# Fill products, per-pair transposes, a halved last product and placed casts in a planned attention and channel-mix kernel

## The chip, the cores and the metric

The kernel runs on one core of a Trainium2 chip. The metric is the device time of one execution in microseconds (us). A core has five engines that work side by side, each through its own queue in order: TensorE (PE, whose weight loads are listed as PEld), VectorE (DVE), ScalarE (ACT), GpSimd (POOL) and SyncE (SP), which here only issues DMA transfers.

## The reference

Blockwise causal attention on 8 batches of 8 heads, 576 positions and 64 columns a head, with blocks of 64 positions, and then an RWKV channel mix on the joined heads:

```python
scores = scale * np.matmul(q, k.transpose(0, 1, 3, 2))
mask = block_i >= block_j                      # blocks of 64 positions
attn = softmax(np.where(mask, scores, -1e9))
x = matmul(attn, v).transpose(0, 2, 1, 3).reshape(8, 576, 512)

x_prev = np.concatenate([zeros, x[:, :-1, :]], axis=1)
xk = mu_k * x + (1.0 - mu_k) * x_prev
xr = mu_r * x + (1.0 - mu_r) * x_prev
k = np.maximum(xk @ w_k, 0.0)                  # 512 -> 1024
v = k * k @ w_v                                # 1024 -> 512
r = 1.0 / (1.0 + np.exp(-(xr @ w_r)))
out = r * v
```

## The kernel before, in words

**A plan.** The kernel body doesn't issue instructions in source order. Each piece of work is a task with an engine, an assumed duration, a rank, a function that issues it, and the tasks and ring buffers that it needs. `Plan.order` steps through a modelled time: whenever an engine is free, it takes the task with the lowest rank whose needs are met, so the order of each engine's queue is fixed when the kernel is built. The ranks and the order of the first loads stand in the table `RANK`. On the chip each queue runs in that order and waits where something isn't ready.

**Attention.** A batch's q and k come in float32, are cast to bf16 and turned so that the 64 columns of a head stand on partitions. For batches 2 to 7 (`add_qk`) a DMA transpose does this (L289). For batches 0 and 1 (`add_long`, `add_long_qkt`) the rows come in long pieces, nine consecutive positions per partition; `add_long` casts them (L336 on ACT, L338 on DVE, L340 on POOL), and `add_long_qkt` has TensorE transpose them (L415), 128 columns at a time, for a group of two head pairs: eight blocks of q, eight of k, and the ninth of both. Three copies then put the positions back in order on their way out of PSUM (L438 on DVE or L436 on ACT, eight positions in a row; L440 on DVE for the ninth). `add_scores` multiplies k and q (L501) for a pair of heads and part of the causal triangle, ACT takes the exponential (L523), POOL zeroes the corners (L531). `add_av` multiplies by V (L562, V carries a column of ones), DVE normalises (L582, L583) into `x`. `add_xt` turns `x` in float32 (L636), and ACT copies it to `xt` (L615).

**Channel mix.** It runs on nine chunks of 512 positions. `add_mix` takes the difference of neighbours (L674, even column blocks on POOL, odd ones on DVE), and DVE makes xk and xr (L686). `add_pk` multiplies by WK (L722, eight products of four matmuls), ACT takes relu (L732), DVE squares (L738). `add_pr` multiplies by WR (L751), ACT takes tanh (L761). `add_pv` multiplies by WV (L774, four products of eight matmuls), DVE joins both (L784), SP stores (L790). Weights are loaded and cast once: WK on POOL (L385), WR and WV on ACT (L387, L390); V is cast on POOL (L365), q and k of batches 2 to 7 on POOL (L261, L273).

**Rings.** The PSUM tiles are `s` (scores, two), `m` (two) and `mm` (two). The float32 staging tiles for q, k and weights are the ring `ld` (ten), for V `vl` (five).

The first 39 loads are issued in the order of `RANK['loads']`; batch 0's attention, then the first chunk's mix, then `add_pk(0, ...)` follow, with batch 1's attention in between. From there on each batch's attention is interleaved with the channel mix of the chunk before. A task for warming TensorE exists, but its count `WARM` is 0.

Of the kernel before, what the change touches and what calls it, by code (L numbers as in the profile page):

```python
# [9 lines left out]
FP = mybir.dt.float32  # L10
# [6 lines left out]
WARM = 0  # L17
# [6 lines left out]
RANK = {  # L24
 'loads': ['g0q', 'g0k', 'g1q', 'v0', 'v1', 'v4', 'wr2', 'g1k', 'v3', 'v2',
           'b1g1k', 'b1g0q', 'wv3', 'b1v1', 'b1g0k', 'wv0', 'wk5', 'b1g1q',
           'wv7', 'b1v0', 'wk0', 'b1v4', 'mu', 'wk2', 'wk4', 'wr1', 'b1v3',
           'wk3', 'wv1', 'wv4', 'wk1', 'wr0', 'b1v2', 'wv5', 'wr3', 'wk7',
           'wk6', 'wv6', 'wv2'],
 'cast k': -19.0,  # L30
 'cast r': -62.5,
 'cast v': 144.5,
 'qkt0': [555.0, -316.5],
 'score0': [-496.5, -428.0, -330.5, -515.0, -325.5, -425.5, -398.0, -322.5,
            -273.0, -575.0, -336.0, -726.5, -776.0],
 'av0': [-630.5, -721.5, -426.0, -327.5, -868.5, -672.0, -382.5, -608.5],
 'xt0': [-181.0, -124.0, -26.0, -319.5, -317.0],
 'mix0': [107.0, 245.5, 354.5, 303.5],
 'pk0': [-175.0, -144.0, -221.0, -320.5, -195.5, -337.0, -157.0, -47.0],
 'pr0': [95.0, 62.0, -196.0, -175.0],  # L40
 'pv0': [104.5, 94.5, -223.5, 81.5],
 'qk': [56.0, 57.0, 63.5, 67.0],
 'v': 67.0,
 'qkt': [267.5, -111.5],
 'turn': -116.0,
 'av': -72.0,
 'xt': 9.5,
 'mix': 840.5,
 'xr': 121.0,
 'moe': 21.5,  # L50
# [3 lines left out]
class Plan:  # L54
# [10 lines left out]
    def add(self, eng, dur, rank, fn, deps=(), takes=(), uses=()):  # L65
        t = {"eng": eng, "dur": dur, "rank": (rank, len(self.tasks)), "fn": fn,
             "deps": [d for d in deps if d is not None], "takes": list(takes),
             "uses": list(uses) + list(takes), "start": None, "end": None}
        for u in t["uses"]:
            u["left"] += 1  # L70
        for u in t["takes"]:
            u["taker"] = t
        self.tasks.append(t)
        return t
# [69 lines left out]
def kernel(  # L144
# [90 lines left out]

    vo_buf = [plan.buf("vo") for _ in range(B)]
# [7 lines left out]
    def add_qk(b, pr, rank, turn_rank):  # L244
        nb = plan.buf("nb")
        for n, src in enumerate((q, k)):
# [10 lines left out]
            def fn(n=n, key=key):  # L257
                if n == 0:
                    tiles["nb", b, pr] = NBs[nbs[0] % len(NBs)]
                    nbs[0] += 1  # L260
                nc.gpsimd.tensor_copy(  # L261
                    tiles["nb", b, pr][:, n, 0:4],
                    tiles[key][:, 0:512].rearrange("p (t c) -> p t c", c=P))
            cast["qk", b, pr, n] = on(
                "POOL", 0.68, rank, fn,
# [11 lines left out]
        last = on("POOL", 0.4, rank, tail, [tl_load[b], cast["qk", b, pr, 0]],  # L277
# [8 lines left out]
        def turn():  # L286
# [8 lines left out]
            "SP", 1.3, turn_rank, turn,  # L295
# [7 lines left out]
    def heads(b):  # L303
# [7 lines left out]
            (1, 0): ("DVE", "POOL"), (1, 1): ("POOL", "DVE")}  # L311

    def add_long(b, g, ranks):


        for n, src in enumerate((q, k)):
# [3 lines left out]
            for x in range(2):  # L320
# [9 lines left out]
                def fn(n=n, key=key, x=x, eng=eng):  # L330
                    if x == 0:
                        tiles["nb", b, g, n] = new("nl", [P, JT, P], BF)
                    dst = tiles["nb", b, g, n][:, :, x * D:x * D + D]
                    src = tiles[key][:, :].rearrange("p (j d) -> p j d", d=D)
                    if eng == "ACT":
                        nc.scalar.copy(dst, src)  # L336
                    elif eng == "DVE":
                        nc.vector.tensor_copy(dst, src)  # L338
                    else:
                        nc.gpsimd.tensor_copy(dst, src)  # L340
                cast["qk", b, g, n].append(on(
                    eng, {"ACT": 0.7, "DVE": 0.5, "POOL": 0.75}[eng],
                    ranks[n], fn, [t] + cast["qk", b, g, n],
                    takes=[] if x else [nb], uses=[ld] + ([nb] if x else [])))
# [9 lines left out]
    def add_v(b, ranks):  # L354
        for sc in range(5):
# [8 lines left out]
            def fn(n=n, sc=sc):  # L364
                nc.gpsimd.tensor_copy(VOs[b % 2][0:n, sc, :, 0:D],  # L365
                                      tiles["vl", b, sc][0:n])
            cast["v", b, sc] = on(
                "POOL", 0.68, ranks[sc], fn, [t],
# [3 lines left out]
    def add_w(name, n, ranks, rank):  # L372
        src = {"k": moe_w_k, "r": moe_w_r, "v": moe_w_v}[name]
        src = src.rearrange("(cc p) (n j) -> n cc p j", p=P, j=C)
        for i in range(n):
# [6 lines left out]
            def fn(i=i, cc=cc, half=half):  # L382
                w = tiles["w", name, i][:, 0:C]
                if name == "k":
                    nc.gpsimd.tensor_copy(WK[:, cc, half * C:half * C + C], w)  # L385
                elif name == "r":
                    nc.scalar.copy(WR[:, i], w)  # L387
                else:

                    nc.scalar.activation(WV[:, i], w, AF.Copy, scale=0.5)  # L390
            cast["w", name, i] = on(
                "POOL" if name == "k" else "ACT", 0.68 if name == "k" else 0.6,
                rank, fn, [t], uses=[ld])


    def add_long_qkt(b, g, rank):
        first = g == 0
        if first:
            tiles["qktbuf", b] = plan.buf("qkt")
        buf = tiles["qktbuf", b]  # L400
        srcs = [tiles["nbbuf", b, g, n] for n in range(2)]
        evs = []
        for part in range(3):
            m = plan.buf("m")
            blocks = ([(part, j) for j in range(JT - 1)] if part < 2
                      else [(0, JT - 1), (1, JT - 1)])
            take = first and part == 0

            def fn(part=part, blocks=blocks, take=take):
                if take:  # L410
                    tiles["qkt", b] = new("qkt", [P, HP, 2, KP], BF)
                tiles["pq0", b, g, part] = new("m", [P, CH], FP)
                pst = tiles["pq0", b, g, part][:, :].bitcast(BF)
                for i, (n, j) in enumerate(blocks):
                    nc.tensor.matmul(  # L415
                        pst[:, i * P:(i + 1) * P], tiles["nb", b, g, n][:, j],
                        identb, is_transpose=True, start=(i == 0),
                        stop=(i == len(blocks) - 1))
            ns = sorted({n for n, j in blocks})
            t = on("PE", 0.06 * len(blocks), rank, fn,  # L420
                   [c for n in ns for c in cast["qk", b, g, n]],
                   takes=[m] + ([buf] if take else []),
                   uses=[srcs[n] for n in ns] + ([] if take else [buf]))

            def ev(part=part, take=take):
                qkt = tiles["qkt", b]
                if take:
                    nc.vector.memset(qkt[:, :, 1, S:KP], 0.0)
                pst = tiles["pq0", b, g, part][:, :].bitcast(BF)
                prs = slice(2 * g, 2 * g + 2)  # L430
                if part < 2:
                    dst = qkt[:, prs, part, 0:S].rearrange(
                        "q y (p j) -> q y p j", j=JT)[:, :, :, 0:JT - 1]
                    src = pst.rearrange("q (j y p) -> q y p j", y=2, p=D)
                    if g == 0 and part == 1:
                        nc.scalar.copy(dst, src)  # L436
                    else:
                        nc.vector.tensor_copy(dst, src)  # L438
                else:
                    nc.vector.tensor_copy(  # L440
                        qkt[:, prs, :, 0:S].rearrange(
                            "q y n (p j) -> q y n p j", j=JT)[
                                :, :, :, :, JT - 1],
                        pst[:, 0:2 * P].rearrange(
                            "q (n y p) -> q y n p", n=2, y=2))
            t = on("ACT" if g == 0 and part == 1 else "DVE",
                   1.35 if part < 2 else 0.4, SOON, ev,
                   [t] + ([] if take else [evac["qkt", b, "zero"]]),
                   uses=[m, buf])
            if take:  # L450
                evac["qkt", b, "zero"] = t
            evs.append(t)
        for y in range(2):
            evac["qkt", b, 2 * g + y] = evs
# [88 lines left out]
    def add_av(b, h, rank):  # L543
# [12 lines left out]
        def fn():  # L556
            if first:
                tiles["x", b, blk] = new("x", [P, 5, P], FP)
            PA = tiles["pa", b, h] = new(ring, [P, CH], FP)
            for mt in range(5):  # L560
# [103 lines left out]
    def add_mix(c, cc, rank):  # L664
# [4 lines left out]
        eng = "DVE" if cc % 2 else "POOL"  # L669

        def fn():
# [5 lines left out]
        sub = on(eng, 0.8 if eng == "DVE" else 1.3, rank, fn,  # L677
                 list(xt_of[c][cc]), takes=[d], uses=[xtbuf[c]])
# [89 lines left out]
    def add_pv(c, jt, rank):  # L768
        m, o = plan.buf("mm"), plan.buf("o")

        def fn():
            ps = tiles["pv", c, jt] = new("mm", [P, CH], FP)
            for jc in range(JCn):
                nc.tensor.matmul(  # L774
                    ps, tiles["k2", c][:, jc, jt * P:(jt + 1) * P], WV[:, jc],
                    start=(jc == 0), stop=(jc == JCn - 1))
# [139 lines left out]
```

The softmax here doesn't subtract the row's maximum and nothing guards it: scores larger than these inputs give would overflow.

## Time and profile before

| what | us |
|---|---|
| median of 4 runs | 277.55 |
| lowest to highest | 277.33 to 280.23 |
| the profiled execution | 277.37 |
| its span, first to last instruction | 275.6 |
| PE busy in the span | 252.2 |
| DVE busy | 213.6 |
| ACT busy | 188.6 |
| POOL busy | 138.0 |

The profile is one execution. Its page gives each engine's busy share in 40 slices of the span, the clock that TensorE was granted, the groups of instructions with their mean durations, and the chain of work that ended last: followed back from the last instruction, at each step to what released it. A matmul's length in it holds the way through the array, so matmuls that follow each other closely overlap in the records; the distance of their starts tells the pace.

### The profile page before, as it was taken

How to read it: one execution, taken by the hardware profiler on the slowest of the kernel's cores; microseconds unless marked ns; L12 is line 12 of the kernel's file. 1: busy time of each engine (PE TensorE's matmuls, PEld its weight loads, DVE VectorE, ACT ScalarE, POOL GpSimd, SP SyncE). 2: the span in 40 equal slices, each digit the busy share in tenths (PEclk: the TensorE clock that was granted, in tenths of full speed). 3: DMA queues.
4: the chain of work that ended last, by engine and by line, in shares of the span. 5: the costliest groups of instructions: out<-in, count | busy, mean ns of one | idle time of the engine just before them, and what ended most of it. 6: DMA issues, size and time to landing. Idle time of an engine off the chain costs nothing.

```text
span 275.6 us, 6287 instructions
## 1 busy us (share of the span) xinstructions
PE 252.2 (92%) x2296; PEld 137.4 (50%) x2296; DVE 213.6 (77%) x362; ACT 188.6 (68%) x297; POOL 138.0 (50%) x299
## 2 busy tenths in 40 slices
PE   1659667999999999999999999999999999999994
PEld 1337532656465546644654566456545655444441
DVE  4556899778889778996899588957994888987641
ACT  2566996976887779786886688668866873460630
POOL 4452695665858454765677567557754302301000
PEclk9999986999999999999999999999999999999999
DMA  7999997698999998999999999999995001202102
GB/s 226 280 301 354 228 348 173 127 204 204 235 194 209 222 252 178 189 226 273 209 172 240 257 199 174 230 275 200 192 221 170 18 0 75 79 0 114 42 38 114
DMA packets 137471, 51.28 MB, mean 186 GB/s; under 512 B 128224, under 2 KB 128224, under 8 KB 137440
## 3 DMA queue, kind: packets, MB, share of 16 engines
q1 hardware_dynamic: 137440, 50.88, 81.6%
q8 instruction: 18, 0.29, 0.5%
q14 instruction: 13, 0.11, 0.1%
HBM read 33.56 MB, written 9.44 MB: 156 GB/s over the span
## 4 chain that ended last, share of the span: by engine, by line
PE 69%; DVE 9%; DMA 6%; ACT 5%; POOL 4%; issue 4%; SPq 1%; POOLq 0%; DVEq 0%; ACTq 0%
PE t_mm L774 20%; PE t_mm L722 18%; PE t_mm L751 9%; PE t_s L501 7%; PE t_m L562 7%; PE t_m L636 5%; ACT t_e L523 3%; DVE t_k L738 3%; DMA t_ld<-in_k_dram 2%; DMA t_qkt<-NB 2%; DMA t_ld<-in_moe_w_k_dram 2%; DVE t_xr L686 1%; PE t_mm L562 1%; POOL WK L385 1%; DVE t_o L784 1%
## 5 line engine op out<-in xcount | busy, mean ns | idle before, releaser
L523 ACT ACTIVATE t_e<-t_s 128x1024 f16<-128x1024 f32 x96 | 96.1, 1026 | 26.2 <-PE t_s L501 24.1
L722 PE MATMUL t_mm<-t_xk,WK 128*128 128x512 f16 x288 | 71.5, 385 | 2.1 <-POOL WK L385 1.9
L738 DVE TENSOR_TENSOR t_k<-t_kr 128x512 f16<-128x512 f32 x72 | 58.9, 833 | 15.2 <-ACT t_kr L732 14.9
L774 PE MATMUL t_mm<-WV,t_k 128*128 128x512 f16 x288 | 66.8, 379 | 0.5 <-DVE t_o L784 0.5
L732 ACT ACTIVATE t_kr<-t_mm 128x512 f32<-128x512 f32 x72 | 43.1, 599 | 15.8 <-PE t_mm L722 15.0
L774 PEld LDWEIGHTS <-t_k 128*128 128x128 f16 x288 | 27.8, 98 | 33.6 <-issue 2.5
L531 POOL MEMSET t_e<- 64x128 f16 x128 | 23.7, 200 | 40.1 <-ACT t_e L523 36.5
L261 POOL CAST NB<-t_ld 128x512 bf16<-128x512 f32 x48 | 34.3, 717 | 16.3 <-DMA t_ld<-in_q_dram 8.4
L722 PEld LDWEIGHTS <-WK 128*128 128x128 f16 x288 | 26.0, 98 | 30.5 <-issue 5.2
L501 PE MATMUL t_s<-t_qkt 64*128 64x64 bf16 (+4 forms) x384 | 35.0, 292 | 6.2 <-DVE t_qkt L440 3.7
L562 PEld LDWEIGHTS <-t_e 128*128 128x128 f16 x896 | 34.6, 99 | 12.0 <-issue 2.3
L784 DVE SCALAR_TENSOR_TENSOR t_o<-t_t,t_mm 128x512 f32<-128x512 f32 x36 | 24.6, 684 | 19.0 <-PE t_mm L774 13.8
L365 POOL CAST VO<-t_vl 128x512 f16<-128x512 f32 (+1 forms) x40 | 28.9, 726 | 17.2 <-DMA t_vl<-in_v_dram 16.0
L751 PE MATMUL t_mm<-WR,t_xr 128*128 128x512 f16 x144 | 36.4, 379 | 0.0
L761 ACT ACTIVATE t_t<-t_mm 128x512 f32<-128x512 f32 x36 | 21.5, 601 | 18.7 <-PE t_mm L751 17.4
L674 POOL TENSOR_TENSOR t_d<-t_xt 128x512 f32<-128x512 f32 x18 | 21.6, 1201 | 23.3 <-ACT t_xt L615 13.4
L562 PE MATMUL t_m<-VO,t_e 128*128 128x65 f16 x784 | 31.8, 193 | 0.1
L686 DVE SCALAR_TENSOR_TENSOR t_xk<-t_d,MUK,t_xt 128x512 f16<-128x512 f32 x36 | 30.4, 859 | 1.6 <-POOL t_d L674 1.3
L686 DVE SCALAR_TENSOR_TENSOR t_xr<-t_d,MUR,t_xt 128x512 f16<-128x512 f32 x36 | 31.2, 880 | 0.0
L615 ACT COPY t_xt<-t_m 128x256 f32<-128x256 f32 (+7 forms) x68 | 23.7, 400 | 10.7 <-PE t_m L636 10.7
L583 DVE TENSOR_TENSOR t_x<-t_m,t_r 128x320 f32<-128x320 f32 x56 | 27.5, 492 | 1.9
L636 PE MATMUL t_m<-identf,t_x 128*128 128x128 f32 x160 | 24.5, 279 | 3.1 <-DVE t_qkt L438 1.3
(44 smaller groups left out, 185.9 us busy)
## 6 DMA issues: line engine op xcount, KB each, us to landing
out_dram<-t_o SPq DMA_DIRECT2D x36, 256.0 KB, 2.9
t_vl<-in_v_dram SPq DMA_DIRECT2D x32, 256.0 KB, 4.2
t_ld<-in_q_dram SPq DMA_DIRECT2D x48, 128.0 KB, 3.5
t_ld<-in_k_dram SPq DMA_DIRECT2D x48, 128.0 KB, 3.3
t_ld<-in_q_dram SPq DMA_DIRECT2D x8, 288.0 KB, 5.1
t_ld<-in_k_dram SPq DMA_DIRECT2D x8, 288.0 KB, 4.9
t_ld<-in_moe_w_v_dram SPq DMA_DIRECT2D x8, 256.0 KB, 4.8
t_ld<-in_moe_w_k_dram SPq DMA_DIRECT2D x8, 256.0 KB, 4.6
```

The lines of the kernel that those rows point to most:

```text
L261: nc.gpsimd.tensor_copy(tiles["nb", b, pr][:, n, 0:4], tiles[key][:, 0:512].rearrange("p (t c) -> p t c", c=P))
L365: nc.gpsimd.tensor_copy(VOs[b % 2][0:n, sc, :, 0:D], tiles["vl", b, sc][0:n])
L501: nc.tensor.matmul(PS[:, h, col:col + n], qkt[rows, pr, 1, kc * P:kc * P + P], qkt[rows, pr, 0, q0:q0 + n], start=True, stop=True)
L523: nc.scalar.activation(tiles["e", b, pr][:, :, i, :], tiles["ps", b, it], AF.Exp, scale=ISQ)
L562: nc.tensor.matmul(PA[:, mt * D1:(mt + 1) * D1], stationary(b, h, kc, mt), VOs[b % 2][:, kc, head, 0:D1], start=(kc == 0), stop=(kc == mt))
L636: nc.tensor.matmul(px[:, i * P:(i + 1) * P], src, identf, is_transpose=True, start=(i == 0), stop=(i == 3))
L686: nc.vector.scalar_tensor_tensor(tiles[name, c][:, cc], tiles["d", c, cc], (MUK1, MUR1)[n][:, cc:cc + 1], tiles["xt", c][:, cc, 1:CH + 1], ...
L722: nc.tensor.matmul(ps, WK[:, cc, jc * P:(jc + 1) * P], tiles["xk", c][:, cc], start=(cc == 0), stop=(cc == CCn - 1))
L732: nc.scalar.activation(tiles["kr", c, jc], tiles["pk", c, jc], AF.Relu)
L738: nc.vector.tensor_tensor(tiles["k2", c][:, jc], KR, KR, ALU.mult)
L751: nc.tensor.matmul(ps, tiles["xr", c][:, cc, jt * P:(jt + 1) * P], WR[:, cc], start=(cc == 0), stop=(cc == CCn - 1))
L774: nc.tensor.matmul(ps, tiles["k2", c][:, jc, jt * P:(jt + 1) * P], WV[:, jc], start=(jc == 0), stop=(jc == JCn - 1))
```

## The change

Five things change at once.

1. 150 tasks of lowest priority (`fill`) are put into the plan on TensorE. Each issues two 128-column products of the identity with itself into a part of a PSUM tile that nothing reads. The plan puts one wherever its model finds TensorE with nothing else to do.
2. `add_long_qkt` transposes per head pair: nine blocks of 64 columns for q and nine for k of each pair. One copy for each puts the nine positions of a partition in order and writes them without a gap. The number of transposes doubles from 72 to 144, and the copies go from 12 to 16.
3. The last product of the last chunk is computed, joined and stored in two halves of 256 columns.
4. A cast or a difference is a task that can stand on one of several engines (`flex`), and a table `RANK['eng']` gives the engine for each by name.
5. The ranks and the order of the first loads are new, and some assumed durations.

In the new program order on TensorE, 82 fill products stand ahead of the first transpose, the other 218 in sixteen places up to the first product of `add_pk`, the last 36 of them one score task ahead of it; none comes later. Of the first loads, the first four transfers are as before; counted in the 39 names of the list, WK's blocks 0 to 3 stand at 19, 15, 25 and 17 (before at 21, 31, 24 and 28), and V of batch 0 is complete at 14 (before at 10). All four differences of the first chunk stand on POOL. Of the casts of q, k and V of batches 2 to 7, 16 move from POOL to ACT and 17 to DVE. Over the kernel the differences on DVE go from 18 to 8.

```diff
-WARM = 0
+FILL = 150
 RANK = {
- 'loads': ['g0q', 'g0k', 'g1q', 'v0', 'v1', 'v4', 'wr2', 'g1k', 'v3', 'v2',
-           'b1g1k', 'b1g0q', 'wv3', 'b1v1', 'b1g0k', 'wv0', 'wk5', 'b1g1q',
-           'wv7', 'b1v0', 'wk0', 'b1v4', 'mu', 'wk2', 'wk4', 'wr1', 'b1v3',
-           'wk3', 'wv1', 'wv4', 'wk1', 'wr0', 'b1v2', 'wv5', 'wr3', 'wk7',
-           'wk6', 'wv6', 'wv2'],
+ 'loads': ['g0q', 'g0k', 'v4', 'b1g0q', 'g1q', 'v2', 'wk4', 'wv3', 'g1k',
+           'wk6', 'b1g1k', 'v0', 'v3', 'v1', 'wk1', 'b1g0k', 'wk3', 'b1v0',
+           'wk0', 'mu', 'wr1', 'b1g1q', 'wk5', 'b1v2', 'wk2', 'wv7', 'wv2',
+           'wk7', 'wv6', 'wv0', 'b1v3', 'wv5', 'wv1', 'wv4', 'b1v1',
+           'b1v4', 'wr0', 'wr3', 'wr2'],
...
+ 'eng': {'v32': 'POOL',
+         'wk7': 'ACT',
+         'qk201': 'DVE',
+         'long0010': 'DVE',
...
+    def flex(key, alts, rank, fn, deps, takes=(), uses=()):
+        eng = RANK["eng"].get(key, next(iter(alts)))
+        t = plan.add(eng, alts[eng], rank, lambda: fn(eng), deps, takes, uses)
+        t["key"], t["alts"] = key, alts
+        return t
+
+    def convert(eng, dst, src, scale=None):
+        if eng == "ACT":
+            if scale is None:
+                nc.scalar.copy(dst, src)
+            else:
+                nc.scalar.activation(dst, src, AF.Copy, scale=scale)
+            return
+        e = nc.vector if eng == "DVE" else nc.gpsimd
+        if scale is None:
+            e.tensor_copy(dst, src)
+        else:
+            e.tensor_scalar_mul(dst, src, scale)
...
     def add_long_qkt(b, g, rank):
...
-                for i, (n, j) in enumerate(blocks):
-                    nc.tensor.matmul(
-                        pst[:, i * P:(i + 1) * P], tiles["nb", b, g, n][:, j],
-                        identb, is_transpose=True, start=(i == 0),
-                        stop=(i == len(blocks) - 1))
...
         for y in range(2):
-            evac["qkt", b, 2 * g + y] = evs
+            evac["qkt", b, 2 * g + y] = []
+            for n in range(2):
+                m = plan.buf("m")
...
+                    for j in range(JT):
+                        nc.tensor.matmul(
+                            pst[:, j * D:(j + 1) * D],
+                            tiles["nb", b, g, n][y * D:(y + 1) * D, j],
+                            identb[y * D:(y + 1) * D, y * D:(y + 1) * D],
+                            is_transpose=True,
+                            start=(j == 0), stop=(j == JT - 1))
...
+                    convert(eng, qkt[:, 2 * g + y, n, 0:S].rearrange(
+                                "q (p j) -> q p j", j=JT),
+                            pst[:, 0:S].rearrange("q (j p) -> q p j", p=D))
...
     def add_pv(c, jt, rank):
...
+        parts = 2 if (c, jt) == (NCH - 1, 3) else 1
+        w = CH // parts
...
+    def fill():
+        ps = tiles["pa last"]
+        for x in range(2):
+            nc.tensor.matmul(ps[:, 384:512], identb, identb, start=True,
+                             stop=True)
...
+    w0 = on("PE", 0.01, SOON, fill_first, [], takes=[wbuf])
+    for i in range(FILL):
+        on("PE", 0.12, 1e6, fill, [w0])
```

## The prediction

> **What bounds the kernel now.** I read the page's slices first, then busy time by stage, then the chain that ended last, then the timeline of the first 50 us, engine by engine.
>
> ```profile
> PE   1659667999999999999999999999999999999994
> ...
> PEclk9999986999999999999999999999999999999999
> ```
>
> A slice is 6.9 us. From the eighth slice on TensorE is full; everything that is loose lies in the first 49 us and in the tail. Busy time by stage (PE, PEld, DVE, ACT, POOL, granted clock, DMA share, GB/s) shows it:
>
> ```profile
> 5.30:25.70 20.40, 14.34 (x144) 9.30 (x146) 11.11 (x17) 11.96 (x14) 8.58 (x22) 1.00 1.10 314
> 25.70:39.30 13.60, 9.66 (x142) 6.88 (x141) 12.62 (x24) 12.10 (x17) 9.08 (x19) 1.00 1.03 280
> 39.30:46.20 6.90, 4.46 (x14) 1.30 (x13) 6.87 (x7) 4.97 (x8) 5.73 (x11) 0.51 0.73 210
> 46.20:250.00 203.80, 201.91 (x1901) 110.38 (x1901) 168.12 (x292) 149.82 (x244) 112.37 (x236) 1.00 0.86 179
> ```
>
> Between 46.2 and 250 us TensorE idles 1.9 us in all. So the end is the moment at which the stream of feed-forward products begins, plus the products left then, plus gaps, plus the tail. That moment stands in the chain:
>
> ```profile
> 39.88 1.37 issue
> 41.67 1.64 POOL WK L385 x2
> 43.36 3.10 PE t_mm L722 x7
> ```
>
> The first product of `add_pk` (L722) ran at 40.89 on the first column block; the second waited until 43.36 for a cast of WK that stood in GpSimd's queue behind a V cast and a 1.48 us subtraction. And it starts slowly: 7 matmuls of 512 columns take 3.10 us. In the timeline the same operation shows TensorE's two speeds:
>
> ```profile
> 8.01 1.22 PE L415 MATMUL t_m<-identb,t_nl 128*128 128x128 bf16 x10 [1.71 <-ACT t_nl L336]
> ...
> 20.01 0.95 PE L562 MATMUL t_mm<-VO,t_e 128*128 128x65 f16 x14
> ...
> 30.21 0.64 PE L562 MATMUL t_mm<-VO,t_e 128*128 128x65 f16 x14
> ...
> 35.60 0.73 PE L415 MATMUL t_m<-identb,t_nl 128*128 128x128 bf16 x10
> ```
>
> Ten transposes took 1.22 us at 8 us and 0.73 us at 35.6 us; taking off one matmul's own length (311 and 216 ns), they follow each other every 0.10 and 0.057 us. The clock column reads 1.00 before 25.7 us, but these durations say that TensorE ran slowly until then.
>
> **What the skill says.** "TensorE: Matmul & The Clock Gate", section "What's actually happening": the array runs at half rate by default and after an idle window of about 3.4 us, at full rate after a busy one. The trace agrees: clock 0.51 from 39.3 to 46.2 us (two windows), after a stretch in which TensorE did little between 35.9 and 39.3. The same page, "Back-to-back issue gap", gives about 81 ns for each pair of a weight load and a 128-column product; this trace's transposes show 57. "SBUF — State Buffer", section "Door 1: The DMA port swizzle", speaks of 16-byte lines, each crossing of which costs. The trace agrees: the copy L440 writes 256 elements, each 18 bytes from the last, in 1288 ns, while L438 writes 1024 in runs of eight in 1225.
>
> **The change, part by part.**
>
> *Fills.* 150 tasks of two identity products stand where the plan saw TensorE idle, 300 products in all: 82 ahead of the first transpose, 218 more before the first `add_pk`, none after. They wait for nothing but `identb` (ready at 1.31) and, once, for a normalisation that the next task needs anyway; but they stand in order, so real work behind them waits. At 0.057 us each they cost 17 us of queue, at 0.10 us 30. I take the clock as raised at 6 us, a busy window after 1.3 us: 47 products by then, 35 x 0.057 = 2.0 after, so the first 82 end at F = 8.0 (7.5 to 9.5, the latter if the clock never rises). The first q rows were cast by 5.26 before, so the first transposes come 2.7 us late.
>
> *Transposes.* 72 of 128 columns become 144 of 64 columns; each still loads 128 columns of weights, so between 0.03 us (the narrow weight loads of L501, four in 0.13 us) and 0.057; I take 0.05. That is 144 x 0.05 = 7.2 against 72 x 0.057 = 4.1, +3.1 us of TensorE, all before the first `add_pk`, where fills would otherwise stand. The ordering copies per group were L438 1.23 + L438 1.23 (or L436 on ACT 1.02) + L440 1.29; now four of 576 elements, contiguous writes: 1225/1024 x 576 = 0.69 us on DVE, about 0.65 on ACT (1016/1024 x 576 plus a start of 0.1). Over two batches DVE gives up 12.6 us for 8 x 0.69 = 5.5, ACT goes from 2.0 to 8 x 0.65 = 5.2.
>
> *The start, walked along the queues.* Loads land about one in 0.8 us in both orders, the first four alike (3.6 to 7.2). The k rows' second cast now stands on ACT behind the first ordering copy. From F: transpose 0.5, release 0.15, copy 0.65, k cast 0.67, release 0.1, two k transposes 1.0, eight fills 0.46: first scores at S = F + 3.5 = 11.5, against 10.7 before. From S to the last exponential of batch 0 ACT has 12 exponentials at their spacing of 0.95 (six took 5.71) = 11.4, four copies 2.6, casts of wv3 and v0 1.2, the small exponential 0.5: 15.7. TensorE has in the same stretch 100 fills 5.7, 12 scores 3.6, the small scores 0.3, 72 transposes 3.6, four AV products 1.8: 15.0. Stepping the two against each other gives 16.4, so E = 27.9; before, it ended at 29.5 (cold products and the idle time 17.0 to 19.4 for L440). V of batch 0 now lands last at about 21 (16.6 before), and its first user comes at S + 12, so it is covered.
>
> From E to the products, VectorE decides. From E + 1.05 (exponential, zeros, the last-but-one AV product) its queue holds: two normalisations 1.4, four xk 3.4, three xr that stand ahead of the last xk 2.55, one cast 0.75, wk2 0.6, two ordering copies 1.4, and ahead of these a wait of 1.0 until TensorE has come to their transposes (E + 7.4): 11.1, so E + 12.1 = 40.0. All of batch 0's subtractions are on GpSimd now (1.2 us each, the last ends at E + 9), and wk0 to wk3 are cast well before (wk2 lands near 31). I allow 1.0 us for the releases I did not count: the stream of products begins at 41.0 (40 to 43.5).
>
> *What that is worth.* 43.4 - 41.0 = 2.4 us; two products of `add_pk` instead of one stand before the wait, 0.2; the products from 43.36 to 46.17 ran at about half rate, which costs 2.8 / 2 = 1.4 us and goes if the fills, 36 of them just ahead of `add_pk`, keep the clock up.
>
> *Last product in halves.* Sixteen products of 256 columns for eight of 512: 1.73 us either way. After the last of them L784 works on 256 columns, about 0.41 for 0.69, and a 128 KB store ends the kernel instead of 256 KB (2.0 us from issue to landing in the trace); between 0.2 and 0.6, I take 0.4.
>
> *Casts placed by the table.* For batches 2 to 7, 20 q/k and 13 V casts leave GpSimd for ACT (16) and DVE (17), and over the kernel 10 subtractions leave DVE for GpSimd. DVE: 17 x 0.72 - 10 x 0.92 = +3; ACT: +10; both against over 35 us free each in the middle stage. I count nothing; TensorE's work hides it. If an order is unlucky, gaps like the present 0.64 us at 143.4 us double: 0 to +4 us, and -1.9 at the very best. GpSimd's scaled cast of wv is not in the trace; between 0.62 (its plain cast) and 1.2 (its subtraction), needed only much later, so nothing.
>
> Sum: 2.4 + 0.2 + 1.4 + 0.4 = 4.4 us off the profiled execution's 277.4 us (span 275.6 plus 1.8 around it; the median of the four runs, 277.55, is the same within noise): 273.0.
>
> **Rivals.**
> *The start is no earlier.* If S or the loads slip, or the DVE queue sees its waits in sequence, the stream begins at 43.4 again; only the clock and the tail are won: 277.4 - 1.8 = 275.6. For it: the first transposes are late by 2.7 us and V by 4. Against: two of the slow waits of the old start (L440, WK) are gone for certain. Chance 0.14.
> *The middle gets new gaps.* All is won at the start and 3 us lost between 46 and 250: 276.0. For it: DVE is 82% busy there and takes more casts. Against: ACT and POOL are loose. Chance 0.08.
> *Short products are dearer than the gaps.* One mechanism: fills and 64-column transposes, 362 of them between F and `add_pk`, stand in TensorE's queue at more than their place. TensorE's own sum from F is 218 x 0.057 + 144 x 0.05 + 21 scores x 0.28 + 8 AV x 0.45 + 5 x 0.58 = 32 us, so F + 32 = 40 is already as late as the DVE chain: every nanosecond on each of the 362 delays the start. At the page's 81 ns, 218 x 0.024 + 144 x 0.031 = 9.7 us, and F 1 us later: 273.0 + 10.7 = 283.7. It overtakes the gain from 4.4 / 362 = 12 ns each. Against: the trace's 57 ns, and 0.03 for narrow loads. Chance 0.12.
> That the clock isn't held is the extreme of this and inside that chance: no window of the trace with such a dense stream stayed slow.
>
> **How the numbers follow.** My forecast 0.66, with its own range 271 to 275.2 (start 40 to 42.5, tail 0.2 to 0.6). The rivals at 275.6 and 276 have 0.22 together, so the range runs from 270.8 to 277.6 and leaves most of the last rival out. A measurement of this kernel tells about 1%, 2.8 us, from no change: below 274.8 lies nearly all of the forecast, 0.65; the middle rivals and its edge are the same, 0.23; the last rival slower, 0.12.
>
> **What would show it.** Right: transposes before 12 us at 0.057 spacing with the first near 8; clock 1.00 from 36 to 49; the first full run of `add_pk` between 40 and 42.5 at 0.216 a product; no WK among its releasers; the last store about 0.4 us sooner after TensorE's end. Wrong: first exponential after 13.5, TensorE without idle time before `add_pk` (fills in the way), or over 3 us idle from 46 to 250.

## The result, and the profile after

| | before | after |
|---|---|---|
| median of the runs, us | 277.73 (63 runs) | 276.41 (42 runs) |
| profiled execution, us | 277.37 | 275.33 |
| its span, us | 275.6 | 273.2 |

The ratio of after to before is 0.9935, 95% interval [0.9918, 0.9951]: 0.65% faster, 1.8 us. Both kernels have a slower state in some executions; the ratio leaves these out, so it isn't that of the medians. The forecast was 4.4 us. Its rival "the middle gets new gaps" (276.0) came nearest.

The page of the changed kernel has the start filled and shows no fall of the clock in this execution:

```profile
PE   8999997999999799999999999999999999999995
...
PEclk9999999999999999999999999999999999999999
```

The same stages as were shown of before (PE, PEld, DVE, ACT, POOL, granted clock, DMA share, GB/s):

```profile
5.30:25.70 20.40, 19.90 (x391) 16.75 (x389) 11.57 (x21) 15.28 (x21) 9.19 (x24) 1.00 1.07 299
25.70:39.30 13.60, 12.93 (x227) 10.90 (x227) 12.16 (x24) 11.99 (x18) 11.00 (x19) 1.00 1.05 314
39.30:46.20 6.90, 5.25 (x48) 2.42 (x46) 5.30 (x9) 6.12 (x10) 6.49 (x10) 1.00 1.11 219
46.20:250.00 203.80, 200.59 (x1890) 109.09 (x1888) 169.03 (x299) 153.12 (x254) 99.42 (x212) 1.00 0.89 180
```

From 39.3 to 46.2 us the clock is 1.00 where it was 0.51. From 46.2 to 250 us TensorE now idles 203.8 - 200.59 = 3.2 us, where it idled 1.9.

The timeline of TensorE shows the fills, the first transposes, the first products of `add_pk`, and two stops (in brackets: idle time before the piece, and what ended it):

```profile
1.36 7.08 PE L996 MATMUL t_mm<-identb 128*128 128x128 bf16 x82 [1.36 <-POOL identb masks.py:199]
8.37 0.60 PE L606 MATMUL t_m<-identb,t_nl 64*128 64x64 bf16 x18
...
39.92 3.00 PE L899 MATMUL t_mm<-t_xk,WK 128*128 128x512 f16 x12
...
44.27 0.23 PE L738 MATMUL t_m<-VO,t_e 128*128 128x65 f16 x2
46.07 0.53 PE L738 MATMUL t_m<-VO,t_e 128*128 128x65 f16 x12 [1.57 <-POOL VO L429]
...
92.79 0.60 PE L812 MATMUL t_m<-identf,t_x 128*128 128x128 f32 x4
95.14 0.61 PE L675 MATMUL t_s<-t_qkt 64*128 64x512 bf16 x6 [1.75 <-DMA t_qkt<-NB]
```

The full run of products begins at 39.92 us, not 43.36, and at full speed: 12 matmuls in 3.00 us. But the attention of batch 1 stops for 1.57 us at 44.5, and batch 3's for 1.75 us at 93.4. The first has its reason in GpSimd's queue:

```profile
37.66 3.22 POOL L431 TENSOR_SCALAR WV<-t_ld 128x512 f16<-128x512 f32 x2
40.95 0.34 POOL L705 MEMSET t_e<- 64x128 f16 x2
41.38 1.54 POOL L431 TENSOR_SCALAR WV<-t_ld 128x512 f16<-128x512 f32 x1
42.97 0.20 POOL L705 MEMSET t_e<- 64x128 f16 x1
43.26 1.68 POOL L431 TENSOR_SCALAR WV<-t_ld 128x512 f16<-128x512 f32 x1
45.00 0.34 POOL L705 MEMSET t_e<- 64x128 f16 x2
45.41 1.17 POOL L429 CAST VO<-t_vl 128x512 f16<-128x512 f32 x2
```

Four casts of WV with the factor 0.5, about 1.6 us each, stand ahead of two casts of batch 1's V, for which TensorE waits. The chain that ended last says the same where it once named WK:

```profile
43.26 1.68 POOL WV L431
...
45.41 0.62 POOL VO L429
46.03 0.04 issue
46.07 0.53 PE t_m L738 x12
```

The second reason is in SyncE's queue (start and time to issue):

```profile
87.47 0.45 SPq L973 DMA_DIRECT2D out_dram<-t_o  x1
87.96 0.43 SPq L406 DMA_DIRECT2D t_vl<-in_v_dram  x1
88.50 3.94 SPq L486 DMA_TRANSPOSE t_qkt<-NB  x1
```

This DMA transpose took 3.94 us to issue (the median of the 24 is 1.66) and landed at 95.09. It brings the rows of batch 3's second pair of heads, which TensorE wanted at 93.39. In the kernel before the same rows had landed at 90.61, and TensorE took them at about the same time, without a stop:

```profile
93.14 0.61 PE L501 MATMUL t_s<-t_qkt 64*128 64x512 bf16 x6
```

The spans add up. The start won 43.36 - 39.92 = 3.4 us. The clock at the first `add_pk` won 1.4 (the forecast's working; the window's clock is 1.00). The tail, from TensorE's last end to the end of the span, went from 275.56 - 271.78 = 3.78 to 273.24 - 270.15 = 3.09, so 0.7. TensorE's gaps from the full run of products on grew from 1.9 to 4.9 us, a loss of 3.0. That makes 2.5 us; the spans differ by 2.3. The small rest is about one matmul, and the kernel before had already run one at 40.89. So 5.5 us were won and over half was lost again.

### The profile page after: what moved, and what is told of

It is laid out like the page before. It is cut to its first block, busy times and chain, and to the rows that moved or that the text cites. A ratio compares the mean times of both kernels' runs of the same rounds, so it can differ in the third digit from the quotient of the medians.

```text
span 273.2 us, 7043 instructions
## 1 busy us (share of the span) xinstructions
PE 262.8 (96%) x2676; PEld 152.6 (56%) x2676; DVE 210.5 (77%) x373; ACT 195.6 (72%) x315; POOL 128.6 (47%) x275
## 4 chain that ended last, share of the span: by engine, by line
PE 81%; DVE 8%; DMA 5%; POOL 3%; ACT 2%; issue 1%; POOLq 0%; SPq 0%; DVEq 0%; ACTq 0%
PE t_mm L957 21%; PE t_mm L899 20%; PE t_mm L928 10%; PE t_m L738 9%; PE t_s L675 8%; PE t_m L812 6%; PE t_mm L996 6%; DMA t_qkt<-NB 2%; DMA MUK<-in_moe_mu_k_dram 2%; POOL WV L431 2%; ACT t_e L697 2%; DVE t_xk L863 2%; DVE t_k L915 1%; DVE t_xr L863 1%; DVE t_x L759 1%
## 5 line engine op out<-in xcount | busy, mean ns | idle before, releaser
L899 PE MATMUL t_mm<-t_xk,WK 128*128 128x512 f16 x288 | 68.9, 380 | 1.2 <-ACT t_kr L909 0.6
L957 PE MATMUL t_mm<-WV,t_k 128*128 128x512 f16 (+1 forms) x296 | 66.9, 373 | 0.0
L915 DVE TENSOR_TENSOR t_k<-t_kr 128x512 f16<-128x512 f32 x72 | 55.1, 775 | 13.3 <-ACT t_kr L909 13.1
L851 POOL TENSOR_TENSOR t_d<-t_xt 128x512 f32<-128x512 f32 x28 | 32.6, 1171 | 16.6 <-DVE t_xr L863 6.9
L738 PEld LDWEIGHTS <-t_e 128*128 128x128 f16 x896 | 32.9, 97 | 12.1 <-issue 2.6
L967 DVE SCALAR_TENSOR_TENSOR t_o<-t_t,t_mm 128x512 f32<-128x512 f32 (+1 forms) x37 | 24.7, 668 | 15.4 <-PE t_mm L957 12.0
L863 DVE SCALAR_TENSOR_TENSOR t_xk<-t_d,MUK,t_xt 128x512 f16<-128x512 f32 x36 | 34.7, 965 | 2.5 <-POOL t_d L851 2.3
L675 PE MATMUL t_s<-t_qkt 64*128 64x64 bf16 (+4 forms) x384 | 32.0, 277 | 2.3 <-DMA t_qkt<-NB 1.8
L675 PEld LDWEIGHTS <-t_qkt 64*128 64x128 bf16 x384 | 12.8, 94 | 19.2 <-issue 11.6
L996 PE MATMUL t_mm<-identb 128*128 128x128 bf16 x300 | 22.0, 234 | 1.6 <-POOL identb masks.py:199 1.4
```

Source lines behind the costliest of these rows:

```text
L675: nc.tensor.matmul(PS[:, h, col:col + n], qkt[rows, pr, 1, kc * P:kc * P + P], qkt[rows, pr, 0, q0:q0 + n], start=True, stop=True)
L738: nc.tensor.matmul(PA[:, mt * D1:(mt + 1) * D1], stationary(b, h, kc, mt), VOs[b % 2][:, kc, head, 0:D1], start=(kc == 0), stop=(kc == mt))
L851: (nc.vector if eng == "DVE" else nc.gpsimd).tensor_tensor(tiles["d", c, cc], x[:, cc, 1:CH + 1], x[:, cc, 0:CH], ALU.subtract)
L863: nc.vector.scalar_tensor_tensor(tiles[name, c][:, cc], tiles["d", c, cc], (MUK1, MUR1)[n][:, cc:cc + 1], tiles["xt", c][:, cc, 1:CH + 1], ...
L899: nc.tensor.matmul(ps, WK[:, cc, jc * P:(jc + 1) * P], tiles["xk", c][:, cc], start=(cc == 0), stop=(cc == CCn - 1))
L915: nc.vector.tensor_tensor(tiles["k2", c][:, jc], KR, KR, ALU.mult)
```

## The experiments

All ratios are to the kernel before, of runs on the same chip. The theories carry letters, and each expectation says what its letters hold; the leading one is that the start's gain was made and then lost in the stops of the middle, above all behind the scaled casts.

### The scaled casts: the factor 0.5 moved into the ReLU

```diff
-                convert(eng, dst, tiles["w", name, i][:, 0:C],
-                        0.5 if name == "v" else None)
+                convert(eng, dst, tiles["w", name, i][:, 0:C])
...
-                                 AF.Relu)
+                                 AF.Relu, scale=0.5 ** 0.5)
```

The ReLU's output is squared next, so a factor of the root of 0.5 in it does the same as 0.5 on WV.

> The changed kernel with the factor 0.5 of WV moved into the relu (scale 0.7071 before the square), so that every WV cast is a plain copy; order and engines are kept. Theory A (the four scaled casts on GpSimd, 1.6 us each, hold up the V cast of batch 1 behind them): a GpSimd cast of WV takes about 0.65 us, the 1.6 us that TensorE stood before the first AV product of batch 1 go, and the time falls by 1.3 to 1.9 us against the changed kernel, to about 274.8, ratio to before 0.989. Rival B (the loads and DMA transposes of batches 2 and 3 are the next bound): the stop at 44.5 us goes, but TensorE waits as much longer for a DMA transpose later on; the time stays within 0.4 us of the changed kernel.

Measured: 274.98 us, ratio 0.9879 [0.9832, 0.9926]. The timeline of TensorE in this kernel, across the place of the first stop:

```profile
44.42 1.04 PE L898 MATMUL t_mm<-t_xk,WK 128*128 128x512 f16 x4
45.30 0.59 PE L737 MATMUL t_m<-VO,t_e 128*128 128x65 f16 x14
```

And its timeline of GpSimd:

```profile
40.42 0.61 POOL L429 CAST WV<-t_ld 128x512 f16<-128x512 f32 x1
41.09 0.20 POOL L704 MEMSET t_e<- 64x128 f16 x1
41.36 0.69 POOL L429 CAST WV<-t_ld 128x512 f16<-128x512 f32 x1
42.11 0.34 POOL L704 MEMSET t_e<- 64x128 f16 x2
43.63 1.78 POOL L429 CAST VO<-t_vl 128x512 f16<-128x512 f32 x2 [1.19 <-DMA t_vl<-in_v_dram]
```

A plain cast takes 0.6 to 0.7 us where the scaled one took 1.6. The V casts now start at 43.63 instead of 45.41, held only by their own load, and the stop at 44.5 us is gone. Batch 1's V products begin at 45.30, though, only 0.8 us sooner than the stop had ended, because in this execution `add_pk` waited 1.04 us for xk at 40.58. The profiled execution itself was long, 278.22 us. Its second stop, at 93.0 us, was 2.13 us long and the clock fell after it, which accounts for about 1.7 us, half of 3.41 (busy times, clock, DMA share and GB/s of the stretch that holds the stop and of the next):

```profile
92.05:95.47 3.42, 1.29 (x13) 0.74 (x11) 1.79 (x3) 0.65 (x2) 0.61 (x1) 1.00 0.86 174
95.47:98.88 3.41, 3.41 (x15) 1.61 (x12) 1.09 (x2) 2.21 (x3) 0.61 (x3) 0.50 0.96 212
```

### The fills: empty, in three surroundings

In the changed kernel `fill` returns at once, with all orders kept:

> The changed kernel with the 150 fill tasks planned as they are but issuing nothing: every other instruction in the same order. Theory A (the fills hold the clock, at the price of a late start): first transposes at 5.3 instead of 8.4 us, first exponential 1 to 2 us earlier than 11.7; but slow products until about 25 us and again around the first add_pk, so that the stream of products begins between 40 and 42 and runs slowly for 3 us: 1.5 to 3.5 us slower than the changed kernel, near 278.5. Rival D (the fills are in the way, other parts carry the gain): equal or faster than the changed kernel, 275 to 276.4.

Measured: 276.18 us, ratio 0.9925 [0.9887, 0.9963], the same as with fills. The trace says why: the first products of `add_pk` run at a lower clock (busy times, clock 0.74, DMA share, GB/s):

```profile
39.30:46.20 6.90, 5.95 (x38) 2.51 (x38) 4.38 (x8) 4.12 (x7) 6.43 (x11) 0.74 1.11 196
```

but batch 1's attention still begins at 45.59 us, since V's casts decide when. The slow clock used up time in which TensorE would have stood. The fills also stood ahead of the products: without them the first product runs at 37.88, 2.0 us sooner. But TensorE then waits 1.00 us for xk and goes on at 39.91, where the run begins in the changed kernel.

The same edit with the scaled casts out of the way:

> e1_half_in_relu (plain WV casts, 0.5 in the relu) with the 150 fill tasks planned but issuing nothing. Theory A2 (the fills do hold the clock at the first add_pk, worth 1.4 us, but with the scaled casts in GpSimd's queue TensorE waited at batch 1's V cast anyway, so that the worth could not be seen): now 0.8 to 1.6 us slower than e1_half_in_relu, near 276.2. Rival D (the fills are worth nothing: what they win in clock they lose by delaying the first transposes by 3 us): within 0.4 us of e1_half_in_relu, near 275.

Measured: 277.52 us, ratio 0.9950 [0.9923, 0.9977], against 0.9879 with fills. Here batch 1's attention begins at 46.50 instead of 45.30, after a stage at half clock (same columns, clock 0.53):

```profile
39.30:46.20 6.90, 5.96 (x21) 1.95 (x21) 5.46 (x8) 3.16 (x5) 3.23 (x7) 0.53 1.19 215
```

So with the scaled casts out of the way the fills are worth about 0.7%, 2 us (the two intervals just overlap); with them nothing showed.

The kernel before with 150 fills put into its plan:

```diff
+    w0 = on("PE", 0.01, SOON, fill_first, [], takes=[wbuf])
+    for i in range(FILL):
+        on("PE", 0.12, 1e6, fill, [w0])
```

> The kernel before with nothing but the 150 fill tasks, planned into its own order. Theory A: granted clock 1.00 throughout, the AV and score products of the first 26 us at full pace, the first add_pk products at 0.216 instead of 0.43 us (1.4 us); the cast of WK still ends near 43 us on GpSimd, so little more than that: 1.2 to 2.5 us faster than before, 275.2 to 276.5. Rival D: the fills ahead of the first transposes delay the start by 1 to 3 us and the gain is eaten: 277 to 279.

Measured: 282.14 us, ratio 1.0166 [1.0130, 1.0202], slower. The last exponential of batch 0 ends at 29.92 us and the full run of `add_pk` begins at 45.71, two microseconds later than before, and a stop of 2.05 us is new at 72.15. The clock is 1.00 up to the products, and falls to half for 3.41 us after that stop. But this is not the old order with fills added. The tasks took places in the plan's modelled time, and the plan ordered the rest anew: the other instructions are the same, yet the queues of ScalarE, VectorE and GpSimd part from those of the kernel before at their 27th to 30th instruction, SyncE's at its 59th. The loss belongs to the fills and that order together; what the fills alone do in the old order was not measured. How much of the 3.4 us at the start belongs to the new order and how much to the transposes per pair isn't known: the transposes alone in the old plan were not tried.

### The tail: the kernel before with the last product in halves

> The kernel before with nothing but the last product in two halves. By the traces the tail from TensorE's end to the end of the span fell from 3.8 to 3.05 us: 0.7 us faster than before, ratio 0.9975. Rival: the halves cost TensorE as much in extra weight loads, 0 to 0.2 us.

Measured: 277.51 us against 278.19 for before, ratio 0.9977 [0.9955, 1.0000]: about 0.6 us, near the 0.7 that the traces show and the 0.4 of the forecast, at the edge of what can be told.

### The start: mu first, and 20 fill tasks less

The loads of mu issued first, on ScalarE's queue, with the factor in the ReLU:

> e1_half_in_relu with the two small loads of mu issued at the very start on ACT's queue instead of in 27th place on SP's. Theory E (VectorE's queue stood until 28.1 us for mu, ahead of the last normalisations of batch 0, and so set the start of the products): mu has landed by 10 us, the wait of 0.8 us and the 1.0 us of its slowed second operation go, add_pk starts 0.8 to 1.8 us sooner, time 0.5 to 1.5 us below e1_half_in_relu. Rival: the start moves, and the time is lost again at 93 us for the late transpose: within 0.4 us.

Measured: 274.85 us, ratio 0.9900 [0.9859, 0.9940]; the first product ran at 40.20. The start didn't move, so mu wasn't its limit. In this kernel's chain the products wait for xk, which stands in VectorE's queue behind a cast of WK whose load landed at 33.61 us.

The first 20 fill tasks empty (42 of the 82 leading products stay), with the factor in the ReLU:

```diff
     def fill():
+        fills[0] += 1
+        if fills[0] <= 20:
+            return
```

> e1_half_in_relu with the first 20 of the 41 fill tasks ahead of the first transpose issuing nothing, so that 42 products stand there instead of 82. They end near 5 us, when the first rows are cast. If the fills' lateness costs (theory D), the first exponential comes at about 9.5 instead of 11.9 us and the time falls by up to 1 us; if mu and the loads set the start (theory E), the first exponential is earlier and add_pk is not: within 0.4 us of e1_half_in_relu.

Measured: 274.23 us, ratio 0.9865 [0.9822, 0.9909]. The first transposes come at 5.68 instead of 8.37 us, the last exponential of batch 0 ends at 26.96, but the first product still runs at 39.89. So the late first transposes cost nothing at the product stream.

The same with the scaled casts left as they are:

> The changed kernel as it is, with the casts of the value weights still scaled on GpSimd, and only the first 20 of the 41 leading fill tasks empty (42 products left). Theory A (the wait for batch 1's V casts behind the scaled casts decides when batch 1 begins, whatever the start does): like the changed kernel, 276.0 to 276.6 us, ratio 0.9925 to 0.9950, with the first products of batch 1's V at 45.5 to 46.2 us. Rival (the 82 leading products themselves cost what the version with the 0.5 in the ReLU gained without 20 of them, 0.8 us): 275.5 us or less, ratio 0.991 or less.

Measured: 276.40 us, ratio 0.9925 [0.9886, 0.9964], with the V stop of 1.57 us at 44.58. Again, nothing shows while that wait is there.

### The stop at 93 us: one cast of batch 3's keys on GpSimd

`'qk311': 'ACT'` becomes `'qk311': 'POOL'`, which brings one DMA transpose forward past a store and a V load in SyncE's queue. Done in four kernels. With the factor in the ReLU and all fills:

> e1_half_in_relu with one cast, that of k of batch 3, pair 1, put back from ACT's queue to GpSimd's; no other instruction changes place but the DMA transpose that needs it. Theory A3 (the 1.8 to 2.1 us that TensorE stands at 93 us come from this cast, which waits 2 us behind exponentials on ACT): the transpose is issued about 2 us sooner, the stop shrinks to below 0.5 us and the time falls by 1 to 1.8 us against e1_half_in_relu, to about 273.5. Rival B (loads and transposes are paced by the DMA engines): the transpose lands no more than 0.5 us sooner, the stop stays, within 0.4 us.

Measured: 275.36 us, ratio 0.9916 [0.9885, 0.9947], no gain. The stop fell to 0.24 us, but six gaps of 0.22 to 0.68 us came at 100 to 185 us.

With 20 fill tasks less as well:

> The kernel with the 0.5 in the ReLU and 20 fill tasks less (274.23 us), with one cast of batch 3's keys moved from ScalarE to GpSimd, which starts its DMA transpose 1.7 us earlier. Theory F: the stop near 92 us goes, but the DMA engines have as much to move as before, so the stops come later: gaps after 46 us sum to 2 to 3 us still, time within 0.6 us of 274.2, ratio 0.984 to 0.989. Rival (the stop at 92 us is one late cast): the 2.1 us are won, 272.0 to 272.7 us, ratio 0.979 to 0.982.

Measured: 273.10 us, ratio 0.9819 [0.9786, 0.9852], the lowest of the versions that store all of their output. The theory of DMA engines (F) expected no gain, its rival 2.1 us; the middle of the ratios is 1.3 us below the version without this edit, though the intervals overlap. F's figure for TensorE's gaps, 2 to 3 us after 46 us, held with 2.25. The timeline of TensorE at 93 us without this edit:

```profile
91.78 0.60 PE L811 MATMUL t_m<-identf,t_x 128*128 128x128 f32 x4
94.48 0.61 PE L674 MATMUL t_s<-t_qkt 64*128 64x512 bf16 x6 [2.10 <-DMA t_qkt<-NB]
```

The same place with it, without a stop:

```profile
92.67 0.60 PE L811 MATMUL t_m<-identf,t_x 128*128 128x128 f32 x4
93.20 0.61 PE L674 MATMUL t_s<-t_qkt 64*128 64x512 bf16 x6
```

In the changed kernel itself, and with 20 fill tasks less:

> The changed kernel with one cast of batch 3's keys moved from ScalarE to GpSimd, nothing else. Theory G (TensorE's own 225 us are the bound, and each stop after the product stream begins adds its length): the stop of 1.75 us at 93.4 us is gone or under 0.5 us, TensorE's gaps after 40 us fall from 4.8 to about 3.3 us, the time falls by 1.2 to 1.8 us against the changed kernel, ratio to before 0.987 to 0.990. Rival H (with TensorE starting this early the waits only move to later transposes, as in the version with the 0.5 in the ReLU and all fills): gaps still sum to 4.3 us or more, ratio 0.992 or more.

> The changed kernel with its scaled casts, with the first 20 fill tasks empty and the same cast moved to GpSimd. Theory G: against the version with 20 fill tasks less (276.40 us, ratio 0.9925) it falls by 0.6 to 1.8 us, to a ratio of 0.986 to 0.990, and stays above the version that has the 0.5 in the ReLU as well (273.1 us, ratio 0.982) by the V cast's wait of 1.6 us, 0.5 to 0.6 per cent. Rival H: 0.992 or more.

Measured: 277.22 us, ratio 0.9927 [0.9896, 0.9959], and 276.82 us, ratio 0.9924 [0.9891, 0.9957]; before ran at 279.28 on this chip. Neither gains on its own: theory G's numbers missed, rival H's held. In the first the waits of TensorE (total, times, longest) are

```profile
PE t_m L738 <- POOL VO L429: 2.9, 3, 1.6
...
PE t_s L675 <- DMA t_qkt<-NB: 0.2, 1, 0.2
```

and in the timeline of TensorE one of the three is a new stop where the changed kernel had none:

```profile
183.41 0.44 PE L738 MATMUL t_m<-VO,t_e 128*128 128x65 f16 x9
185.00 0.31 PE L738 MATMUL t_m<-VO,t_e 128*128 128x65 f16 x5 [1.15 <-POOL VO L429]
```

The scaled casts are what tells these versions apart. With and without them, the rest equal, the ratios are 0.9935 and 0.9879 (all fills), 0.9925 and 0.9865 (20 less), 0.9924 and 0.9819 (20 less and this cast moved). Three pairs, all one way, the last with intervals apart. The traces go the same way: with scaled casts the V products of batch 1 go on at 46.1 to 46.4 us in four profiles, with plain casts and fills they begin at 44.7 to 45.3 in six.

### The DMA engines: 18 stores left out

> The kernel with the 0.5 in the ReLU and 20 fill tasks less (274.23 us), with the stores of the first three row tiles of output chunks 1 to 6 left out, so those outputs are not written: 18 stores of 256 KB, 4.7 MB, some 22 us of all 16 DMA engines at the 210 GB/s that the middle of the profile shows. All orders are kept. Theory F (from 46 us on TensorE has caught up with the DMA engines, and the landing of the transposed rows sets its pace): the last transposes of batch 3 and batch 7 land earlier than 96.2 and 204.8 us, the stop near 92 us shrinks from 2.1 to under 0.5 us, TensorE's gaps after 46 us sum to under 1.5 us, and the time falls by 2 to 3 us to 271.2 to 272.2 us, ratio to before 0.976 to 0.982. Rival (TensorE's own instructions set the pace, the stops are local): the time stays within 0.6 us of 274.2, ratio 0.984 to 0.989.

Measured: 273.09 us, ratio 0.9814 [0.9780, 0.9848], 1.4 us below the version with the stores by the ratios; the 18 parts of the output are not written. In the timeline of TensorE the stop shrank by more than half:

```profile
92.25 0.60 PE L811 MATMUL t_m<-identf,t_x 128*128 128x128 f32 x4
93.79 0.61 PE L674 MATMUL t_s<-t_qkt 64*128 64x512 bf16 x6 [0.94 <-DMA t_qkt<-NB]
```

The last DMA transpose of batch 7 landed 2.5 us sooner (202.3 for 204.8), but TensorE ended only 0.55 us sooner (268.39 for 268.94). So theory F is half right at most: of the 1.16 us by which the stop shrank, 0.69 is the transpose landing earlier (93.74 for 94.43) and 0.47 TensorE coming later, and the landing of the transposes doesn't pace TensorE over the whole middle.

> The kernel before with the same 18 stores left out. Theory F: TensorE of the kernel before starts its products 3.4 us later and so always has a backlog against the DMA engines; its gaps after 43 us sum to 1.9 us, so it can win little: 276.7 to 277.7 us, ratio 0.996 to 1.000. Rival (DMA traffic slows this kernel too, by shared bandwidth rather than by TensorE having caught up): it falls as far as the changed one, by 2 us or more, ratio 0.993 or less.

Measured: 277.82 us, ratio 0.9993 [0.9970, 1.0015]. The same 4.7 MB less bring the kernel before nothing. In the profile of before, TensorE waited 0.17 us in all for DMA transposes after 46 us; its only stops of over 0.3 us, at 143.4 and 203.5, were behind VectorE.

## Why the prediction was right in its start and wrong in its sum

**The bound.** Right. From the first product of `add_pk` to TensorE's last end, less the gaps, there are 225.0 to 226.3 us in every profile of a version with fills and the new order whose clock held (225.4 in the changed kernel, 225.1 in the best); where the clock fell after a stop, 227.1 and 227.2. What is left to differ is the start of the stream and the gaps.

**The start.** Right. First transposes at 8.37 us for 8.0, first exponential at 11.71, E 27.21 for 27.9, the product stream at 39.92 for 41.0 (3.4 us won for 2.4). The extra 1 us is in part luck of the profiled execution. In eight of the ten profiles with fills and the new order two matmuls of `add_pk` ran, then TensorE waited 0.5 to 1.2 us for xk, and the full run came at 40.7 to 41.6 us: the 41.0 of the forecast, and its path through VectorE. Of the short products, the 64-column transposes cost less than taken: 18 took 0.53 us, 0.029 each for 0.05. The fills went as forecast: 47 by the rise of the clock at 6.28, 0.107 us apart, and 0.056 apart after it. So the dear-short-products rival fell. The sign "TensorE without idle time before `add_pk` (fills in the way)" did come true, with 0.2 us idle between 30.4 and 39.9. Without fills the first product came 2 us sooner, but the full run at 39.91 and 40.24 us, after its wait for xk.

**Clock and tail.** Right: 1.00 where it was 0.51, which the forecast put at 1.4 us, and 0.7 us at the tail for 0.4. The fills' share shows by itself only once the V wait is out of the way. The forecast took the fall of the clock in the kernel before for one after an idle window; the stretch ahead of it, 35.94 to 39.35, was idle for 1.75 of 3.41 us.

**The scaled cast: the step that failed.** The forecast put GpSimd's scaled cast of WV "between 0.62 (its plain cast) and 1.2 (its subtraction), needed only much later, so nothing". It took 1.54 to 1.70 us; four of them are 6.4 us of GpSimd's queue. And the WV tile's own late use was the wrong question: what counts is what stands behind the cast, here two V casts that batch 1's attention needs at 44.5 us. Both sides of that wait had moved. Before, batch 1's last V cast ended at 44.38 us and TensorE began the V products at 48.67, a slack of 4.3 us; now the two casts ended at 46.02 and 46.58, and TensorE came at 44.50. With plain casts in the same place this stop goes, and the kernel gains 0.6% to 1.0% more.

**The middle: the second term mis-sized.** "I count nothing; TensorE's work hides it" held for the busy times and not for the order. The forecast allowed 0 to +4 us in its range and took 0; it was +3.0 in the profile. The V stop of 1.57 us and the stop of 1.75 us at 93 us are more than that together; other gaps shrank. In these profiles the stop at 93 us isn't owed to the earlier start. TensorE wanted the rows of batch 3's second pair at 93.39 us and before had taken them at 93.14; what moved is their landing, from 90.61 to 95.09. By the new ranks this pair is transposed third and no longer second, one of its casts stands on ScalarE, a store and a V load stand ahead of the transpose, and its issue took 3.94 us. Moving that cast back, and with it the transpose ahead of the store and the V load, brought the landing to 89.9 us in the best version and to 93.0 in the changed kernel; the new order of the pairs and the long issue were not tried apart. The forecast's own mark of failure, "over 3 us idle from 46 to 250", came true with 3.2.

**What became of the 4.4 us.** With the factor in the ReLU, 20 fill tasks less and one cast moved, the kernel is at 0.9819, about 5 us below before: the size forecast was there, behind two waits that it had costed at nothing. What isn't settled is why moving the one cast helped only there: in three other versions the stop at 93 us went too, and in two of those other gaps of about the same sum took its place; in the third, with gaps of 3.7 us, the time didn't fall either.

## What to carry to other kernels

When a start is made earlier and queues are reordered at the same time, take each later wait from the old profile, note when each of its two sides comes, and give it its slack. A wait that never showed may be exactly as far away as the gain: batch 1's V had 4.3 us, and a TensorE 4.2 us sooner and casts 1.6 us later used up more than that. Follow the order of the transfers too: one transposed pair landed 4.5 us later while every engine's busy time looked harmless. Price a moved cast by what is queued behind it, not by when its own result is read, and don't take a plain cast's time for one with a factor. And test a filler's worth in the final order, with the other waits removed: here it was nothing or about 2 us, by what stood next to it. Where a plan orders the queues, look at whether the added tasks have reordered the rest.

## What the runs showed of the hardware

- GpSimd's float32 to float16 cast of 128 x 512 took 0.6 to 0.7 us plain and 1.62 us with a factor; the scaled one took 0.43 us on VectorE and 0.64 on ScalarE. The groups of WV's casts in the changed kernel (shortest, median and longest in ns, first and last start in us):

```profile
L431 POOL TENSOR_SCALAR WV<-t_ld x4: 1539/1616/1698, 37.7 to 43.3; 128x512 f16<-128x512 f32 x4
L425 ACT ACTIVATE WV<-t_ld x2: 622/642/662, 15.5 to 50.8; 128x512 f16<-128x512 f32 x2
L431 DVE TENSOR_SCALAR WV<-t_ld x2: 417/426/435, 41.1 to 42.0; 128x512 f16<-128x512 f32 x2
```

- The clock fell after stops of TensorE of 2.13 us (the version with the factor in the ReLU) and of 2.05, 2.20 and 2.52 us in three others; after one of 2.10 us in the version with the factor in the ReLU and 20 fill tasks less, and after the 1.75 us of the changed kernel, it held at 1.00. The Trainium skill, "TensorE: Matmul & The Clock Gate", section "What's actually happening", speaks of an idle window of about 3.4 us; here a shorter stop was enough. What tells the cases apart is where the stop lies. In each trace all changes of the clock are whole multiples of 3.41 us apart (6.72, 95.47 and 98.88 us in the version with the factor in the ReLU). Each of the four stops lay wholly inside one such step, and half clock followed for the next. A boundary at 94.05 cut the stop of 2.10 us in two, so that the step before it was idle for only 3.42 - 1.75 = 1.67 us:

```profile
90.63:94.05 3.42, 1.75 (x11) 0.89 (x8) 2.35 (x4) 0.91 (x3) 0.86 (x1) 1.00 1.18 130
94.05:97.46 3.41, 2.98 (x20) 1.50 (x22) 1.11 (x3) 2.21 (x3) 0.59 (x3) 1.00 1.06 225
```

  Idle time alone doesn't give a sharp limit. A step idle for 1.75 us in the kernel before (35.94 to 39.35) was followed by half clock, and so were steps idle for only 1.42 and 1.62 us ahead of the first products in the two versions with empty fills.
- 64-column transposes, each with its own load of 64 x 128 weights, follow each other every 0.029 us in the changed kernel, half the 0.057 of the 128-column ones in the kernel before at full clock.
